# Attention and expert MoE on one core: a 128-column stationary tile for block 0's fold, and keys requested ahead of queries

## The chip, the cores and the metric

The kernel runs as one program on one core of a Trainium2 chip. The metric is the device time of one execution in microseconds (us); lower is better. The figure of the kernel before is the median of three runs.

## The reference

Block-causal attention for 8 batches of 8 heads (576 tokens, head dimension 64, blocks of 64 tokens), and behind it a mixture of 8 experts, each token through the one expert that its gate picks:

```python
scores = scale * np.matmul(q, k.transpose(0, 1, 3, 2))
mask = (pos[:, None] // 64) >= (pos[None, :] // 64)
attn = softmax(np.where(mask, scores, -1e9))
x = np.matmul(attn, v)               # heads side by side: 4608 x 512
expert_idx = np.argmax(x @ w_gate, axis=1)
for e in range(8):
    out[mask_e] = gate_w * (relu(x[mask_e] @ w1[e]) @ w2[e])
```

Everything is float32.

## The kernel before

The attention works on **pairs** of heads: 32 pairs, four to a batch. A pair's 576 queries are split into block 0 (the first 64 tokens, which see only themselves) and four tiles of 128 queries, numbered 1 to 4. The two heads of a pair lie on the two halves of the partitions.

A software pipeline runs the steps of several pairs together. The text `ORDER` lists the steps of one **turn**, each with a lag: `S4:2` in turn t is step S4 of pair t-2. Every engine executes its own steps in the order of this list; the tile framework adds the semaphore waits. A turn is one pair's worth of work; there are 32 and a few to fill and drain the pipeline. The list is written out by hand, and nothing reorders it. Letters:

- **ld** (`op_ld`, L98 to L108): three DMA requests on SP's queue, for the pair's queries `qd` (352 KB, three buffers), its keys `kd` (288 KB, two buffers) and its values `v` (352 KB, five buffers). A request is held on the queue until its buffer is free, and what stands behind it in the queue is held with it. The buffer of `qd` was last read by S0 of three pairs earlier, early in the same turn; that of `kd` by cK and lK of two pairs earlier, the latter in the turn before.
- **cK, lK, cQ, lQ**: keys and queries are split into a rounded part (`kh`, `qh`, ScalarE, that is ACT) and a rest (`kl`, `ql`, VectorE, that is DVE). cK of a pair comes late in the turn of its ld; lK and cQ come in the next turn, lQ, q0 and the scores S4 in the one after.
- **S1 to S4** (L202): scores, in three products each. S4 writes the banks `xa` and `xb`, S1 to S3 write `ya` and `yb`. `xa` and `ya` share one buffer of PSUM, as do `xb` and `yb`: S2, the first of the three in the order, waits until **E4A**, the exponentials read from `xa`, is done.
- **K, M, E**: masking and row maximum (DVE), exponentials (ACT, L234, which end with a read of the accumulator). **T** and **H**: transposes on PE (L270, L273) and their copies out of PSUM. Ta1 needs the exponentials of its pair, E3A last among them.
- **V0 to V5** (L304): products with the values, 64 columns of stationary tile for each head. V5 belongs to block 0. **O** and **O0** copy the results to SBUF.
- **F1, F2, F0** (L339, L333): the **fold**. Each multiplies the transposed output of a pair, as the stationary tile, with 144 columns: an identity, which turns the output back, and the gate's weights for the pair's rows. F1 and F2 take two tiles of 128 columns each; F0 takes block 0's 64 columns. In the trace every float32 product appears as two instructions, so F1 and F2 are four each and F0 two.
- **X, Y** (L348, L358): DVE scales the fold's results on their way to SBUF. F0 opens a new use of the PSUM bank that F1's results lie in, and so it waits until X1 and **Y1** have read them. F2 shares F0's bank.
- **z** and **y**: the router's small steps for the batch before, spread over the turns (DVE, POOL, and a few small products on PE).

The end of a turn on PE is, in order: Tk0, Tb2, F1, Tb1, Ta2, F0, F2, S2, S1, S3, Tx3, Tt0, V0, V2, and in the next turn V1, V3, V4, V5, Ta1, S0, S4.

Behind the attention, from about 370 us on, the experts' products run with an order and semaphores of their own; the change doesn't touch them. At the very start, `__init__` issues ld for pairs 0 and 1, clears constants, and runs seven products on the identity.

Of the kernel before, what the change touches and what calls it, by code (L numbers as in the profile page):

```python
# [8 lines left out]
F32 = mybir.dt.float32  # L9
# [9 lines left out]
P = 128  # L19
H = 8  # L20
S = 576
D = 64
# [14 lines left out]
FC = P + 2 * E  # L37


class Attention:  # L40
# [8 lines left out]
    def __init__(self, ctx, tc, ident, qT, kT, vt, w_gate, ends, po):  # L49
        self.tc, self.nc = tc, tc.nc  # L50
        self.qT, self.kT, self.vt = qT, kT, vt
        self.po = po

        self.ends = ends.rearrange("p (i c) -> p i c", c=P)
        self.M = qT.shape[0] * H // 2
        nc = self.nc
        cp = ctx.enter_context(tc.tile_pool(name="acst", bufs=1))
        self.raw = ctx.enter_context(tc.tile_pool(name="araw", bufs=3))
        self.rawk = ctx.enter_context(tc.tile_pool(name="arawk", bufs=2))
        self.rawv = ctx.enter_context(tc.tile_pool(name="arawv", bufs=5))  # L60
        self.spl = ctx.enter_context(tc.tile_pool(name="aspl", bufs=2))
        self.pt = ctx.enter_context(tc.tile_pool(name="apt", bufs=9))
        self.sm = ctx.enter_context(tc.tile_pool(name="asm", bufs=3))
        self.ot = ctx.enter_context(tc.tile_pool(name="aot", bufs=2))
        self.xp = ctx.enter_context(tc.tile_pool(name="axp", bufs=2))
        self.ps = ctx.enter_context(tc.tile_pool(name="psa", bufs=1, space=PSUM))
        self.ps_t = ctx.enter_context(tc.tile_pool(name="pst", bufs=2, space=PSUM))

        self.cp, self.ident = cp, ident
        self.raws, self.qs = {}, {}  # L70
        self.pb, self.sums, self.neg, self.rs = {}, {}, {}, {}
        self.bank, self.ptile, self.ph, self.oT, self.xs = {}, {}, {}, {}, {}
        self.small_bank, self.at = (None, None), {}
        self.used = {}
        self.op_ld(0)
        self.op_ld(1)
        self.zero = cp.tile([P, D], F32, tag="zero", name="zero")
        nc.vector.memset(self.zero, 0.0)

        self.h0 = [cp.tile([P, P], F32, tag=f"h0{i}", name=f"h0{i}") for i in range(2)]  # L80
        for t in self.h0:
            nc.gpsimd.memset(t, 0.0)
        self.p0 = {}

        t = self.ps_t.tile([P, 512], F32, tag="pt", name="early")
        for _ in range(7):
            nc.tensor.matmul(t[:, 0:P], ident, ident, start=True, stop=True)

        self.fold = cp.tile([P, H // 2, FC], F32, tag="fold", name="fold")
        nc.vector.memset(self.fold, 0.0)  # L90
        nc.scalar.copy(self.fold[:, :, 0:P], ident[:, None, :].to_broadcast([P, H // 2, P]))
        wg = w_gate.rearrange("(m j d) e -> j d m e", d=D, j=2)
        for j in range(2):
            nc.sync.dma_start(self.fold[D * j : D * j + D, :, P + E * j : P + E * j + E], wg[j])
# [3 lines left out]
    def op_ld(self, m):  # L98

        nc = self.nc  # L100
        b = m // 4
        qd = self.raw.tile([P, QS], F32, tag="qd", name=f"qd{m}")
        kd = self.rawk.tile([P, S], F32, tag="kd", name=f"kd{m}")
        v = self.rawv.tile([P, VS, D], F32, tag="v", name=f"v{m}")
        nc.sync.dma_start(qd, self.qT[b, m % 4])
        nc.sync.dma_start(kd, self.kT[b, m % 4])
        nc.sync.dma_start(v, self.vt[b, m % 4])
        self.raws[m] = (qd, kd, v)  # L108

# [201 lines left out]
        self.copy(engine)(t, self.banks(m, "o"))  # L311

    def op_O0(self, m, engine):
        t = self.oT[m, 1] = self.ot.tile([P, D], F32, tag="oT0", name=f"oT0{m}")
        self.copy(engine)(t, self.at["V5", m])

    def out(self, b):
        if b not in self.xs:
# [10 lines left out]
    def op_F(self, m, n):  # L329

        mm, w = self.nc.tensor.matmul, self.fold[:, m % 4]
        if n == 0:
            mm(self.part(2, m, "F0", 2 * FC, 3 * FC)[0:64], self.oT.pop((m, 1)), w, start=True, stop=True)  # L333
            return
        self.part(n, m, n, 0, 2 * FC)
        t = self.rows(m, n)
        for i in range(2):
            o = P * (2 * n - 2 + i)
            mm(t[:, i], self.oT[m, 0][:, o : o + P], w, start=True, stop=True)  # L339
# [1051 lines left out]
```

## Time and profile before

| | |
|---|---|
| median of 3 runs | 837.51 us (837.16 to 837.9) |
| profiled execution, its own time | 834.95 us |
| its span, first to last instruction | 833.2 us |
| PE busy | 812.3 us, 97% of the span |
| ACT, DVE, POOL busy | 554.4, 420.5, 355.4 us |
| mean granted clock of TensorE | 0.995 |

The span is 1.75 us shorter than the profiled execution's own time, and that execution is 2.6 us faster than the median of the runs that were only timed. Busy shares are means over two stages: the attention (to about 366 us) and the experts. In the table of rows below, "idle before" is the time in which the engine did nothing ahead of an instruction, and the name behind the arrow is what ended it; PEld is the load of a stationary tile, which can overlap products.

### The profile page before, as it was taken

The page shows a single profiled execution, that of the slowest core. Times are in us where ns is not written, and L with a number is a line of the kernel's source. Part 1 is how long each engine was busy: PE and PEld are TensorE (multiplying, and loading weights), DVE is VectorE, ACT ScalarE, POOL GpSimd, SP SyncE. Part 2 cuts the span into 40 slices and gives each one's busy share as a digit, 9 for nine tenths or more (in the row PEclk, how much of TensorE's full clock was granted, in tenths as well). Part 3 has the DMA queues.
Part 4 walks back from the last instruction along what each step waited for, and adds up shares of the span by engine and source line. Part 5 has one row for each costly group of instructions (what it writes and reads, how often), then busy time and mean ns, then how long its engine had stood idle before and what let it go on. Part 6 is the DMA issues. An engine that isn't in the chain of part 4 may idle for free.

```text
span 833.2 us, 16492 instructions
## 1 busy us (share of the span) xinstructions
PE 812.3 (97%) x5126; PEld 631.0 (76%) x5126; DVE 420.5 (50%) x1208; ACT 554.4 (67%) x1254; POOL 355.4 (43%) x390
## 2 busy tenths in 40 slices
PE   5999999999999999989999999999999999999996
PEld 4777767777777767767888888888888888888884
DVE  5677787777877877748804400045646544000000
ACT  6888988889888888834554555455546554554552
POOL 2000133222223512244855645466666655544553
PEclk8999999999999999999999999999999999999999
DMA  5225656546363529143946523246766853133212
GB/s 204 82 98 150 166 134 169 124 138 142 121 138 106 142 79 255 35 120 116 284 104 167 167 59 77 76 135 170 236 185 173 267 152 74 43 76 76 67 48 67
DMA packets 83707, 108.81 MB, mean 131 GB/s; under 512 B 45601, under 2 KB 48929, under 8 KB 83618
## 3 DMA queue, kind: packets, MB, share of 16 engines
q1 hardware_dynamic: 38082, 78.26, 31.9%
q0 software_dynamic: 7520, 19.97, 8.1%
q10 hardware_dynamic: 38016, 9.44, 6.9%
q8 instruction: 50, 0.82, 0.4%
q14 instruction: 39, 0.32, 0.1%
HBM read 76.76 MB, written 21.98 MB: 118 GB/s over the span
## 4 chain that ended last, share of the span: by engine, by line
PE 89%; DVE 2%; POOL 2%; ACT 2%; issue 1%; DMA 0%; ACTq 0%; POOLq 0%; DVEq 0%
PE py L1057 23%; PE o L936 12%; PE ph L936 12%; PE o L304 11%; PE o L339 4%; PE ya L202 4%; PE xa L202 3%; PE yb L202 2%; PE px L895 2%; PE pt L1018 2%; PE o L333 1%; ACT pb L234 1%; PE o L190 1%; DVE neg L219 1%; DVE w L1186 1%
## 5 line engine op out<-in xcount | busy, mean ns | idle before, releaser
L1057 PE MATMUL py<-w,low 128*128 (+1 forms) x912 | 226.9, 398 | 0.8 <-ACT low L1009 0.8
L1057 PEld LDWEIGHTS py<-w,low 128*128 128x128 f32 x912 | 168.8, 188 | 38.1 <-issue 1.2
L1180 DVE CAST w<-raw 128x1024 fp32r<-128x1024 f32 x60 | 48.1, 849 | 179.6 <-PE o L936 128.1
L247 POOL TENSOR_SCALAR p<-p,rs 128x64 f32<-128x64 f32 x32 | 14.2, 445 | 257.2 <-DVE rs L243 154.9
L1037 POOL TENSOR_TENSOR low<-h,low 128x512 fp32r<-128x512 f32 x72 | 107.1, 1491 | 21.2 <-ACT h L1010 21.0
L914 POOL TENSOR_TENSOR xl<-xf,xh 128x512 fp32r<-128x512 f32 x38 | 52.0, 1369 | 110.7 <-ACT xf L908 110.6
L1186 DVE TENSOR_TENSOR w<-raw,w 128x1024 fp32r<-128x1024 f32 x60 | 83.9, 1455 | 0.0
L905 ACT CAST xh<-px 128x512 fp32r<-128x512 f32 x38 | 22.3, 588 | 90.9 <-PE px L895 90.9
L936 PE MATMUL ph<-w,xh 128*128 x280 | 75.8, 393 | 0.0
L936 PE MATMUL o<-w,xh 128*128 x280 | 75.8, 393 | 0.0
L983 ACT COPY h<-ph 128x1024 uint16<-128x1024 uint16 x36 | 36.4, 1012 | 45.3 <-PE ph L936 24.0
L974 ACT ACTIVATE h<-o 128x512 f32<-128x512 f32 x37 | 22.2, 600 | 61.8 <-PE o L936 48.2
L936 PEld LDWEIGHTS ph<-w,xh 128*128 128x128 f32 x280 | 52.6, 188 | 11.9
L936 PEld LDWEIGHTS o<-w,xh 128*128 128x128 f32 x280 | 52.6, 188 | 11.7
L1081 POOL DMA_INDIRECT out<-y,idx x35 | 38.0, 1085 | 41.0 <-issue 36.8
L234 ACT ACTIVATE pb<-ya,neg 128x320 f32<-128x320 f32 (+2 forms) x93 | 48.6, 533 | 2.5 <-PE pt30x L273 1.8
L877 POOL DMA_INDIRECT xg<-xd,idx x37 | 45.1, 1220 | 10.4 <-POOL idx L873 10.4
L234 ACT ACTIVATE pb<-yb,neg 128x320 f32<-128x320 f32 (+2 forms) x93 | 49.5, 548 | 0.0
L731 POOL DMA_INDIRECT tab<-toks,posi x40 | 41.8, 1044 | 15.1 <-issue 14.6
L339 PE MATMUL o<-fold,oT 128*128 128x144 f32 x256 | 45.4, 300 | 0.9 <-ACT oT L311 0.6
L1001 ACT COPY h<-hf 128x1024 uint16<-128x1024 uint16 x36 | 43.3, 1203 | 4.1 <-DMA hf<-h 4.0
L219 DVE TENSOR_REDUCE neg<-ya 128x1 f32<-128x320 f32 (+2 forms) x93 | 44.8, 481 | 1.0 <-ACT pb L234 0.9
(965 smaller groups left out, 2122.5 us busy)
## 6 DMA issues: line engine op xcount, KB each, us to landing
raw<-w SPq DMA_DIRECT2D x60, 512.0 KB, 5.4
qd<-qT SPq DMA_DIRECT2D x32, 352.0 KB, 2.9
v<-vt SPq DMA_DIRECT2D x32, 352.0 KB, 4.4
kd<-kT SPq DMA_DIRECT2D x32, 288.0 KB, 3.8
xd<-xt SPq DMA_DIRECT2D x7, 1026.0 KB, 11.3
xd<-xg SPq DMA_DIRECT2D x9, 256.5 KB, 6.9
xg<-w SPq DMA_DIRECT2D x8, 256.0 KB, 10.8
xd<-x SPq DMA_DIRECT2D x8, 128.0 KB, 6.5
```

The source lines that it names most:

```text
L202: ins = mm(out, q[x][r, 128 * (i - 1) : 128 * i], q[y][r, o : o + w], start=n == 0, stop=n == 2, skip_group_check=True,)
L219: ins = self.nc.vector.tensor_reduce(self.neg[m][:, c : c + 1], src, AX.XY if i == 4 else AX.X, ALU.max, negate=True)
L234: ins = self.nc.scalar.activation(dst, src, AF.Exp, bias=self.neg[m][:, c : c + 1], scale=1.0, accum_out=self.sums[m][:, c : c + 1])
L304: self.nc.tensor.matmul(out[r], self.raws[m][2][:, slot], self.ph[m, bank][:, c0:c1], start=t in (0, 5), stop=t in (4, 5), skip_group_chec ...
L339: mm(t[:, i], self.oT[m, 0][:, o : o + P], w, start=True, stop=True)
L877: pool.indirect_dma_start(out=self.xg[i], out_offset=None, in_=self.xd[:, :], in_offset=bass.IndirectOffsetOnAxis(ap=self.idx[:, t : t + 1 ...
L914: pool.tensor_sub(self.xl, self.xf, self.xh).then_inc(sem["xp"], 1)
L936: m = pe.matmul(self.ph[f], x[:, P * k : P * k + P], weights(k, f, part), start=start and k == 0, stop=stop and k == 3,)
L1037: engine.tensor_sub(hl, self.hf if t < 2 else self.h[f], hh).then_inc(sem["hp"], 1)
L1057: m = pe.matmul(self.py[t % 2], h[:, c // 4, P * (c % 4) : P * (c % 4) + P], wf[:, bass.ds(off + (base + 512 * c), 512)], start=n == 0, st ...
L1180: dve.tensor_copy(hi, raw[m % nr]).then_inc(sem["wh"], 1)
L1186: dve.tensor_sub(lo, raw[m % nr], hi).then_inc(sem["wd"], 1)
```

## The change

Three things. A pair of constant SBUF tiles `o0` (128x128, cleared once by GpSimd, that is POOL) takes the place of the rotating 128x64 tile that O0 writes; O0 fills its first 64 columns. F0 takes all 128 columns of it as its stationary tile and so writes 128 rows of PSUM, of which Y0 still reads the first 64. And in `op_ld` the request for the keys goes ahead of that for the queries.

```diff
         self.h0 = [cp.tile([P, P], F32, tag=f"h0{i}", name=f"h0{i}") for i in range(2)]
-        for t in self.h0:
+        self.o0 = [cp.tile([P, P], F32, tag=f"o0{i}", name=f"o0{i}") for i in range(2)]
+        for t in self.h0 + self.o0:
             nc.gpsimd.memset(t, 0.0)
...
+        nc.sync.dma_start(kd, self.kT[b, m % 4])
         nc.sync.dma_start(qd, self.qT[b, m % 4])
-        nc.sync.dma_start(kd, self.kT[b, m % 4])
         nc.sync.dma_start(v, self.vt[b, m % 4])
...
     def op_O0(self, m, engine):
-        t = self.oT[m, 1] = self.ot.tile([P, D], F32, tag="oT0", name=f"oT0{m}")
-        self.copy(engine)(t, self.at["V5", m])
+        t = self.oT[m, 1] = self.o0[m % 2]
+        self.copy(engine)(t[:, 0:D], self.at["V5", m])
...
         if n == 0:
-            mm(self.part(2, m, "F0", 2 * FC, 3 * FC)[0:64], self.oT.pop((m, 1)), w, start=True, stop=True)
+            mm(self.part(2, m, "F0", 2 * FC, 3 * FC), self.oT.pop((m, 1)), w, start=True, stop=True)
             return
```

## Rows read from the trace of the kernel before

**Rows 1.** Busy time by stage, 100 to 200 us: us, then each engine, clock, DMA.

```profile
100.00:200.00 100.00, 99.11 (x839) 71.00 (x837) 78.02 (x299) 87.27 (x249) 29.82 (x40) 1.00 0.60 142
```

**Rows 2.** PE's waits to 360 us: total us, times, longest (the longest wait).

```profile
PE pt0a L273 <- ACT pb L234: 5.4, 1, 5.4
```

**Rows 3.** Chain that ended last, 140 to 164 us: start, us, what.

```profile
141.05 0.34 PE ya L202
...
149.38 0.49 PE o L339 x4
...
150.76 0.39 PE o L333 x2
151.15 0.69 PE o L339 x4
151.84 0.34 PE ya L202
...
163.61 0.34 PE ya L202
```

**Rows 4.** Timeline of a common turn: start, us, instruction, idle before it.

```profile
194.61 0.18 DVE L358 TENSOR_TENSOR lg<-o,rs 128x32 f32<-128x32 f32 x1
...
194.98 0.46 PE L333 MATMUL o<-fold,oT 128*64 128x144 f32 x2
...
195.57 0.22 ACT L234 ACTIVATION_READ_ACCUMULATOR pb<-xa,neg 128x1 f32 x1
...
196.05 0.18 PEld L202 LDWEIGHTS ya<-kh,qh 64*128 64x128 f32 x1
```

**Rows 5.** Timeline, DVE and PE, a turn in which Y1 is late.

```profile
106.51 0.18 DVE L358 TENSOR_TENSOR lg<-o,rs 128x32 f32<-128x32 f32 x1
...
106.84 0.43 PE L333 MATMUL o<-fold,oT 128*64 128x144 f32 x2
```

**Rows 6.** Timeline, PE, the last F1, which opens its bank.

```profile
364.94 0.61 PE L339 MATMUL o<-fold,oT 128*128 128x144 f32 x3 [0.33 <-DVE lg L358]
```

**Rows 7.** Timeline of a turn in which ACT has a router step.

```profile
337.11 0.19 ACT L234 ACTIVATION_READ_ACCUMULATOR pb<-xa,neg 128x1 f32 x1
...
337.41 0.18 PEld L202 LDWEIGHTS ya<-kh,qh 64*128 64x128 f32 x1
```

**Rows 8.** Timeline of the turn after a router step on ACT.

```profile
85.52 0.22 ACT L234 ACTIVATION_READ_ACCUMULATOR pb<-xa,neg 128x1 f32 x1
...
86.17 0.18 PEld L202 LDWEIGHTS ya<-kh,qh 64*128 64x128 f32 x1
```

**Rows 9.** Timeline, PE, Ta1 of pair 13.

```profile
158.05 0.66 PE L273 MATMUL pt13a<-ident,pb 128*128 128x128 f32 x4 [0.56 <-ACT pb L234]
```

**Rows 10.** Timeline, ACT, the same turn.

```profile
154.79 0.67 ACT L119 CAST kh<-kd 128x576 fp32r<-128x576 f32 x1 [1.79 <-DMA kd<-kT]
...
157.77 0.22 ACT L234 ACTIVATION_READ_ACCUMULATOR pb<-ya,neg 128x1 f32 x1
```

**Rows 11.** Timeline, ACT, cK in a common turn.

```profile
187.00 0.67 ACT L119 CAST kh<-kd 128x576 fp32r<-128x576 f32 x1 [0.49 <-PE yb L202]
```

**Rows 12.** Timeline, ACT, cK in the turn of pair 8.

```profile
110.48 0.67 ACT L119 CAST kh<-kd 128x576 fp32r<-128x576 f32 x1 [1.52 <-DMA kd<-kT]
```

**Rows 13.** Timeline, SP's queue: the keys that rows 10 wait for.

```profile
147.96 0.38 SPq L106 DMA_DIRECT2D kd<-kT  x1
```

**Rows 14.** Timeline of the start.

```profile
4.25 0.54 POOL L131 TENSOR_SCALAR q<-qd 128x128 f32<-128x128 f32 x1
...
4.85 0.67 ACT L119 CAST kh<-kd 128x576 fp32r<-128x576 f32 x1 [1.24 <-DMA kd<-kT]
...
5.42 0.62 ACT L116 ACTIVATE qh<-qd 128x512 fp32r<-128x512 f32 x1
...
8.58 0.67 ACT L119 CAST kh<-kd 128x576 fp32r<-128x576 f32 x1 [2.53 <-DMA kd<-kT]
```

**Rows 15.** Busy time by stage, 11.90 to 18.73 us (columns as in rows 1).

```profile
11.90:18.73 6.83, 4.22 (x23) 3.83 (x24) 3.34 (x11) 4.57 (x16) 0.00 (x0) 0.50 0.25 78
```

## The prediction

> **What bounds the kernel now.** I read the page first, then the stages, PE's waits, the chain of work that ended last, and the timeline around each touched step. In the attention PE is busy 99 us of 100, ACT 87 and DVE 78 [rows 1]. PE's longest wait is 5.4 us at the very start [rows 2]; those behind it are short. So in the steady turns PE sets the pace, and a nanosecond that its queue loses counts unless ACT or DVE ends a wait at the same place. The experts' stage behind it is bound by PE too and is not touched: it starts earlier by what the attention gains.
>
> Busy doesn't mean at peak. In the chain, F1 passes in 0.49 us for four instructions, 0.1225 each, but F0 takes 0.39 for two, and F2, the same work as F1, takes 0.69 [rows 3]. All stream 144 columns. F1 follows transposes with 128 columns of stationary tile; F0 has 64, and F2 has 128 again. The excess is 0.39 - 0.245 = 0.145 at F0 and 0.69 - 0.49 = 0.20 at F2: 0.345 us a turn at two changes of shape.
>
> The Trainium skill (TensorEngine Tiling (Array Packing), "Key Properties") says that a change of tiling mode drains TensorE. By that rule alone the change would give back the whole excess, 0.345 us a turn; the rows agree on where it lies, and the next part shows why I take less.
>
> **F0, step by step.** The copy O0 moves the same 64 columns, and F0 streams the same 144. Its wait doesn't go: it still opens the bank that Y1 reads last. In a common turn Y1 ends at 194.61 + 0.18 = 194.79, F0 starts 0.19 later and takes 0.46 to the end of its second instruction: 0.65 after Y1 [rows 4]. In a turn with Y1 late the start comes 0.15 after it (106.69 to 106.84), and F0 takes 0.43: 0.58 [rows 5]. So 0.15 is what the wait itself costs, and F0 hangs on DVE, not only on PE.
>
> With 128 columns and the wait in place, the nearest row is the last F1, which opens its bank behind a late Y: three instructions in 0.61, so two in 0.61 - 0.12 = 0.49 [rows 6], against 0.43 for the narrow one: the wide tile's load comes too late to be hidden. New F0: 0.15 + 0.49 = 0.64 after Y1. A common turn gains 0.65 - 0.64 = 0.01 there, a late one loses 0.06. F2 then follows without a change of shape and gains its 0.20. The change of shape into S2 stays. Sum: **0.21** us in a common turn, **0.14** where Y1 is late.
>
> **What comes late next.** S2 writes the buffer that E4A reads. E4A's last instruction ends at 195.79 and S2's load starts at 196.05, 0.26 later [rows 4]. The least distance that I find between such an end and PE's start is 0.06 (157.99 to 158.05, where PE did wait [rows 9, 10]), so S2 can move up by **0.20**, a hair less than the gain. In the seven turns in which ACT carries the router's exponential (the rows show the last) the end is 0.11 ahead [rows 7], and only **0.05** can be had. In the seven turns after those it is 0.43 ahead [rows 8], no limit; Y1 is late there behind a router step.
>
> Of the 32 turns, 30 lie where PE sets the pace. By kind: 14 common x 0.20 = 2.8; 7 with the router's exponential x 0.05 = 0.35; 7 after them and 2 more with Y1 late, 9 x 0.14 = 1.3. Sum **4.5 us**. Upper bound, if the wide load were hidden in spite of the wait: the same limits at S2, but 0.345 in the nine, 2.8 + 0.35 + 3.1 = 6.3. Lower bound, if the excess isn't the change of shape: only the later wide load is left, -0.06 x 30 = 1.8 us slower.
>
> ACT behind S2: it waits 0.49 us for PE ahead of cK in a common turn [rows 11]; PE's gain of 0.20 eats less than half. DVE is less busy than ACT [rows 1]. I cost the two extra clears on POOL at nothing: they run at the start while ACT waits 1.24 us for keys [rows 14]; without that cover they would delay the identity and PE's warm-up, which feeds nothing.
>
> The rule that speaks against the change is in the Trainium skill, TensorE: Matmul & The Clock Gate, "LDWEIGHTS (loading the stationary operand)": the load's time goes with the columns, P / 1.2 ns, so 64 more cost some 53 ns, an estimate from that page. If both loads of F0 were exposed in 30 turns that is 3.2 us, where my sum has 1.8 from the rows, and counts it already in each turn.
>
> **Keys first, steady turns.** In two turns cK waits for the keys' DMA: 1.79 us and 1.52 us [rows 10, 12], where a common turn waits 0.49 for PE [rows 11]. ACT is 1.30 and 1.03 us late. In the first, Ta1 then waits for ACT [rows 9], and the turn takes 163.61 - 151.84 = 11.77 us against 151.84 - 141.05 = 10.79: 0.98 lost, 0.32 absorbed [rows 3]. By the same absorption the other loses at most 0.71; Ta1's wait there is short, so I take 0.5. Together 1.5 us.
>
> With keys first, the request no longer stands behind the queries', which wait for S0 early in the turn. It needs lK of the turn before, which the trace has done before S2 begins, at 141.05 there [rows 3], so it could go out some 6.9 us ahead of its 147.96 [rows 13]; it needed 154.79 - 147.96 = 6.8 us to land amid the batch's row writes, and is wanted at 154.79 - 1.30 = 153.5. Landing near 141.05 + 6.8 = 147.9 leaves 5 us to spare, unless the writes, issued just before, hold it. Behind it on the queue stand queries and values, neither delayed: the queries still go when S0 is done, and are read a turn later. Bounds 0 and 1.7; I take **1.3**.
>
> **Keys first, start.** ACT begins with cK of pair 0 at 4.85, waiting for keys requested second; the queries, requested first, had landed by 4.25 (POOL reads them then) [rows 14]. Swapped, cK starts near 4.25 and cQ near 4.9, when the queries land, against 5.42: 0.5 earlier. Pair 1's keys, for which ACT waits 2.53 us [rows 14], come earlier likewise, and the exponentials behind that copy with them: some 0.9 at the end of PE's 5.4 us wait. But PE then works at the lower granted clock, 0.50 of full, which is 1.2 GHz, until 18.73 [rows 15]; if the rise comes at the same moment, time won ahead of it is worth half. Bounds 0 and 1.0; I take **0.7**.
>
> **Sum.** 4.5 + 1.3 + 0.7 = 6.5 us. The profiled execution (834.95, of it 833.2 span, 1.75 around it) would take 828.45, its span 826.7. The median of the runs shown is 2.55 above the profiled one; the same 6.5 off it: 837.5 - 6.5 = **831.0 us**.
>
> **Rivals.**
>
> - *The wide load hides behind the transposes after all.* F1 shows 0.1225 per instruction throughout [rows 3]; against it stands the wait for Y1, seen in common and late turns alike. Fold 6.3, keys 2.0: 837.5 - 8.3 = 829.2 us. This is what the rule on draining, named above, comes to under the limit at S2.
> - *Late keys don't set those turns, or the row writes hold the keys as before, and the start's gain is lost to the clock.* For it: the keys would queue right behind the writes. Then only the fold counts: 837.5 - 4.5 = 833.0 us.
> - *The fold gains nothing: the excess is the wait for Y1, not the shape, and the load's lateness is added.* Against it: F2 waits for nothing new and still takes 0.20 more than F1. Fold -1.8, keys +2.0: 837.3 us, no change.
> - *Slower.* The same mechanism, at F0 in each turn, with keys that bring nothing: 837.5 + 1.8 = 839.3 us. It decides if F2 keeps 0.69 in the chain while F0 grows from 0.39 to 0.45. By the page's figure for the load it would be 840.7.
>
> **How the numbers follow.** The forecast has 0.62, with its own range of 829 to 832.5; the first rival 0.10, the second 0.16, the third 0.08, slower 0.04. A measurement of this kernel can tell about 0.2%, 1.7 us, from no change. Forecast and first two rivals are faster by more (0.88, with a little of the third: 0.89), the third within (0.07), the last slower (0.04). The range of 827.5 to 834.0 holds the first three with the bounds of keys and start (the best of all, 6.3 + 1.7 + 1.0, is 828.5); it leaves out 0.12 and the tails.
>
> **What the profile after would show.** F0 as 128*128, 0.64 after Y1; F2 at 0.49 in the chain; the first F2 instruction as short as the others; S2 within 0.05 to 0.1 of E4A's end in common turns, which says that ACT has become the limit there. ACT's waits for kd's DMA gone behind the start; PE's first long wait ending some 0.9 us sooner. The prediction is wrong if F2 keeps 0.69, if F0 ends later than 0.7 after Y1, if ACT's gap ahead of cK closes to nothing in common turns, or if cK waits for keys as long as now.

## The result, and the profile after

Median of four runs 829.75 us (828.45 to 832.52), beside 837.34 (835.52 to 837.9, four runs) for the kernel before: 7.6 us less. The ratio over all runs, which is not quite that of the two medians, is 0.9919 with a 95% interval of 0.9897 to 0.9941. Forecast were 831.0 us and a range of 827.5 to 834.0. A second series of the same kernel (`again`, below) gave 0.99.

The profiled execution took 832.52 us (span 830.8), the longest of its four, so I compare stretches of the two traces, not their ends. From the second S2 to the last one that ORDER times (31.63 to 342.73) the attention takes 311.1 us; before it was 316.2 (32.13 to 348.35). This stretch holds 29 of the forecast's 30 turns; the one ahead of it went from 10.78 to 10.56. The common turn went from 10.77 to 10.58 us.

Busy time by stage of the kernel after, columns as in [rows 1]:

```profile
100.00:200.00 100.00, 99.70 (x869) 73.89 (x866) 79.41 (x302) 89.27 (x256) 28.90 (x39) 1.00 0.60 145
```

PE is still busy throughout; ACT rose from 87 to 89 us of 100, because the same work is done in less time. The chain that ended last, where [rows 3] had 0.49, 0.39 and 0.69 for F1, F0 and F2:

```profile
136.28 0.49 PE o L340 x4
...
137.67 0.37 PE o L334 x2
138.04 0.49 PE o L340 x4
138.53 0.35 PE ya L203
```

F2 now passes in F1's 0.49. A common turn on the timeline, against [rows 4]:

```profile
190.80 0.18 DVE L359 TENSOR_TENSOR lg<-o,rs 128x32 f32<-128x32 f32 x1
...
191.12 0.48 PE L334 MATMUL o<-fold,o 128*128 128x144 f32 x2
...
191.76 0.22 ACT L235 ACTIVATION_READ_ACCUMULATOR pb<-xa,neg 128x1 f32 x1
...
192.03 0.18 PEld L203 LDWEIGHTS ya<-kh,qh 64*128 64x128 f32 x1
```

Y1 ends at 190.98. F0 starts 0.14 later and ends 0.62 after Y1; S2's load starts 1.05 after Y1, where it was 1.26, and 0.05 after E4A's end (191.98), where it was 0.26. The turn that carries the router's exponential, and the one after, against [rows 7] and [rows 8]:

```profile
73.88 0.19 ACT L235 ACTIVATION_READ_ACCUMULATOR pb<-xa,neg 128x1 f32 x1
...
74.12 0.18 PEld L203 LDWEIGHTS ya<-kh,qh 64*128 64x128 f32 x1 [0.31 <-ACT pb L235]
...
84.45 0.22 ACT L235 ACTIVATION_READ_ACCUMULATOR pb<-xa,neg 128x1 f32 x1
...
84.94 0.18 PEld L203 LDWEIGHTS ya<-kh,qh 64*128 64x128 f32 x1
```

The distance to E4A is 0.05 in the first (before 0.11) and 0.27 in the second (before 0.43). The turn that ends at the first of these S2s went from 10.77 to 10.74, the one that ends at the second from 10.94 to 10.82, and the next from 10.78 to 10.56.

The timeline of ACT and SP, against [rows 10 to 13]: cK in the two turns with late keys (108.37 and 151.37), the queue ahead of the second, and cK in a common turn (183.17):

```profile
108.37 0.67 ACT L120 CAST kh<-kd 128x576 fp32r<-128x576 f32 x1 [0.84 <-PE yb L203]
...
136.32 0.61 SPq L582 DMA_DIRECT2D xd<-xt  x1
...
138.69 0.75 SPq L106 DMA_DIRECT2D kd<-kT  x1
...
151.37 0.67 ACT L120 CAST kh<-kd 128x576 fp32r<-128x576 f32 x1 [0.89 <-PE pt12x L274]
...
183.17 0.67 ACT L120 CAST kh<-kd 128x576 fp32r<-128x576 f32 x1 [0.29 <-PE yb L203]
```

In the second the keys are requested 9.3 us sooner than at 147.96 (6.5 us, counted from the turn's S2), but the batch's row write `xd<-xt` (1 MB) was issued 2.4 us ahead of them on the same queue. The row writes' packets (2052 bytes each) run from 137.39 to 149.93, the keys' own (2304 bytes each) begin only at 145.57, and the semaphore on which cK waits for them moves last at 151.29: 12.6 us after the request, and just before cK starts. So the view's name for what ended this wait, PE, is not the whole of it. The forecast had them landed 6.8 us after the request. Counted from the turn's S2, cK starts 2.3 us behind it (151.37 - 149.11), where it was 3.0 (154.79 - 151.84) and a common turn has 1.7. The two turns took 10.75 and 11.02, before 11.35 and 11.78.

The start, against [rows 2], [rows 14] and [rows 15]: PE's longest wait, in the view of waits, the first copies on the timeline, and the busy time at the lower clock:

```profile
PE pt0a L274 <- ACT pb L235: 5.7, 1, 5.7
```

```profile
3.85 0.67 ACT L120 CAST kh<-kd 128x576 fp32r<-128x576 f32 x1 [0.23 <-DMA kd<-kT]
4.67 0.63 ACT L117 ACTIVATE qh<-qd 128x512 fp32r<-128x512 f32 x1 [0.16 <-DMA qd<-qT]
...
8.10 0.67 ACT L120 CAST kh<-kd 128x576 fp32r<-128x576 f32 x1 [2.79 <-DMA kd<-kT]
```

```profile
11.82:18.65 6.83, 4.64 (x25) 4.25 (x26) 3.44 (x9) 4.52 (x17) 0.00 (x0) 0.50 0.41 137
```

cK of pair 0 starts 1.0 us sooner, cQ 0.75, cK of pair 1 0.48. PE's wait grew, because it begins sooner; it ends at 14.01 against 14.51. S2 of the first turn comes only 0.29 sooner.

One thing stands against the gain. At the experts' start PE waits 2.56 us for `xl`, where the trace before had 0.3, and the stretch around its end has a granted clock of 0.50, 1.2 GHz (a row of PE's waits before; after, a row of the timeline and one of busy time by stage):

```profile
PE ph L936 <- POOL xl L914: 0.3, 1, 0.3
```

```profile
398.00 1.22 PE L937 MATMUL ph<-w,xl 128*128 x2 [2.56 <-POOL xl L915]
```

```profile
397.51:400.92 3.41, 2.92 (x7) 2.34 (x8) 3.41 (x3) 0.42 (x1) 3.41 (x3) 0.50 0.88 266
```

The experiments return to it.

### The profile page after: what moved, and what is told of

It is laid out like the page before. It is cut to its first block, busy times and chain, and to the rows that moved or that the text cites. A ratio compares the mean times of both kernels' runs of the same rounds, so it can differ in the third digit from the quotient of the medians.

```text
span 830.8 us, 16466 instructions
## 1 busy us (share of the span) xinstructions
PE 808.1 (97%) x5126; PEld 634.0 (76%) x5126; DVE 420.8 (51%) x1208; ACT 554.8 (67%) x1254; POOL 357.0 (43%) x392
## 4 chain that ended last, share of the span: by engine, by line
PE 87%; issue 3%; POOL 2%; ACT 2%; DMA 1%; DVE 1%; POOLq 1%; DVEq 0%; SPq 0%; ACTq 0%
PE py L1058 23%; PE o L305 12%; PE ph L937 12%; PE o L937 12%; PE ya L203 6%; PE xa L203 3%; PE o L340 3%; PE px L896 2%; PE pt L1019 2%; PE o L334 1%; ACT pb L235 1%; POOL tab L732 1%; PE o L191 1%; DMA out<-y,idx 0%; PE o L1359 0%
## 5 line engine op out<-in xcount | busy, mean ns | idle before, releaser
L1038 POOL TENSOR_TENSOR low<-h,low 128x512 fp32r<-128x512 f32 x72 | 105.2, 1464 | 24.7 <-ACT h L1011 24.7
L1082 POOL DMA_INDIRECT out<-y,idx x35 | 39.8, 1138 | 41.0 <-issue 37.0
L220 DVE TENSOR_REDUCE neg<-yb 128x1 f32<-128x320 f32 (+2 forms) x93 | 41.9, 478 | 3.3 <-ACT pb L235 1.3
```

What stands on the lines that cost most here:

```text
L220: ins = self.nc.vector.tensor_reduce(self.neg[m][:, c : c + 1], src, AX.XY if i == 4 else AX.X, ALU.max, negate=True)
L1038: engine.tensor_sub(hl, self.hf if t < 2 else self.h[f], hh).then_inc(sem["hp"], 1)
```

## The experiments

Theory: the fold gives some 4 us through F2's change of shape and is held by E4A at S2; the keys give something of 1 to 2 us by removing two late landings. Rivals: the keys carry most of it; or they carry nothing. All kernels compute the whole reference. Three series ran, each on one chip beside its own runs of the kernel before: medians 841.41 us (23 runs) in the first, 840.92 (17) in the second, 839.99 (10) in the third; the second and third ran on the same chip. The table puts them together: the ratio to the kernel before over all runs, ACT's wait for the keys' DMA behind the start (total, times, longest, as the view of ACT's waits has it), and the stretch from the second S2 to the last, both in the one profiled execution.

| kernel | median us | ratio (95%) | wait for keys, us | stretch, us |
|---|---|---|---|---|
| before, first profile | | | 3.3, 2, 1.8 | 316.2 |
| `before_again` (one run) | 844.59 | | 8.9, 3, 4.4 | 323.3 |
| `again` | 833.15 | 0.99 (0.9872 to 0.9928) | 3.4, 2, 1.8 | 312.8 |
| `fold_only` | 839.11 | 0.997 (0.9951 to 0.999) | 8.2, 5, 3.7 | 317.8 |
| `keys_only` | 836.11 | 0.9932 (0.9907 to 0.9957) | 2.2, 2, 1.3 | 315.4 |
| `keys_start` | 841.5 | 0.9977 (0.9951 to 1.0004) | 10.0, 5, 4.1 | 320.0 |
| `keys_early` | 829.6 | 0.9877 (0.985 to 0.9904) | none | 310.8 |
| `both` | 830.39 | 0.9877 (0.9851 to 0.9902) | none | 309.7 |
| `f0_with_v` | 838.95 | 0.9976 (0.9952 to 1.0001) | 1.1, 2, 0.8 | 315.8 |
| `narrow_keys_early` | 835.07 | 0.9942 (0.9924 to 0.996) | none | 315.0 |
| `narrow_f2_first` (one run) | 831.6 | | none | 313.8 |

**First series: the change once more, and its parts.** `again` is the changed kernel.

> The changed kernel once more, for a second profile. In its first profile the attention ends 5.6 us sooner than before (the first product behind it, sxl, at 360.6 against 366.2), but PE then waits 2.56 us for xl at 398 where it waited 0.29 before, and the granted clock falls there for 3.4 us. Theory: that wait is a matter of one execution, and the attention's 5.6 us is the change; then this profile has S2 of the 30th turn again near 342.7 and no such wait, a span near 828, and the time lies near 829.7. Rival: the wait belongs to the change (the experts start at another moment against their weights' DMA); then it is here again, and the span is near 830.8.

833.15 against 841.41: 8.3 us. At the experts' start there was no long wait for `xl`. But keys were late in two turns, 11.72 and 11.76 us long, and ACT waited for them as long as in the first profile of the kernel before (3.3 us, two times):

```profile
ACT kh L120 <- DMA kd<-kT: 3.4, 2, 1.8
```

So the swap doesn't always remove the late landings.

`fold_only` keeps the queries first:

```diff
-        nc.sync.dma_start(kd, self.kT[b, m % 4])
         nc.sync.dma_start(qd, self.qT[b, m % 4])
+        nc.sync.dma_start(kd, self.kT[b, m % 4])
```

> The 128-column tile for block 0's fold, with queries requested ahead of keys as before. Theory: a common turn takes 10.58 us as in the changed kernel, against 10.77; the two turns with late keys keep their wait of some 1.5 to 1.8 us for kd's DMA and take 11.2 and 11.6; the start is as before (first Ta1 at 14.5). Some 4.2 us of the gain, 833 us. Rival: the keys carry most of the gain, and the fold alone gives under 2 us: above 835.

The common turn is 10.58, as in the full change, but the time is only 2.3 us under the kernel before. The view of ACT's waits has late keys in five turns:

```profile
ACT kh L120 <- DMA kd<-kT: 8.2, 5, 3.7
```

One turn takes 16.02 us, another 12.40. Late keys alone don't explain why the gain is under the fold's 4 us, since the kernel before has them too: whether the fold's shorter turns make them later is not shown.

`keys_only` is the kernel before with the requests swapped, so the 64-column tile stays:

```diff
+        nc.sync.dma_start(kd, self.kT[b, m % 4])
         nc.sync.dma_start(qd, self.qT[b, m % 4])
-        nc.sync.dma_start(kd, self.kT[b, m % 4])
```

> Keys requested ahead of queries, with the 64-column tile as before. Theory: common turns 10.77 as before, the two turns with late keys shorter by 0.4 to 0.6 us each, first Ta1 at 14.0 instead of 14.5 and 0.3 us kept of that at the first S2 (21.07 against 21.36): 1.3 us in all, 836.0 us. Rival: over 3 us, below 834.5, with the fold's part smaller by as much.

5.3 us faster, with the common turn at its old 10.78. So by the medians the keys gave more than the fold here, though the two intervals just overlap; "something of 1 to 2 us" fell. ACT's waits:

```profile
ACT kh L119 <- DMA kd<-kT: 2.2, 2, 1.3
```

`keys_start` has the fold, and keys first for the first two pairs alone:

```diff
+        pair = [(qd, self.qT[b, m % 4]), (kd, self.kT[b, m % 4])]
+        for dst, src in pair[::-1] if m < 2 else pair:
+            nc.sync.dma_start(dst, src)
```

> The changed kernel, but keys go ahead of queries for pairs 0 and 1 alone, whose loads stand ahead of everything; all later pairs as before. Theory: the start as in the changed kernel (first Ta1 at 14.0, first S2 at 21.1), the two turns with late keys as before the change (11.2 and 11.6): 1.0 us slower than the changed kernel, 830.8. Rival: the early request of later pairs' keys is worth nothing, since the batch's row writes hold them either way: then it equals the changed kernel within 0.3 us in the profile's turns.

A plain miss: 841.5 us, and no gain of the start can be seen (PE's first wait ends at 14.51, S2 comes at 21.59). The waits for keys are back, 10.0 us in five turns. What the swap is worth lies mainly in the steady turns; from `fold_only` the intervals can't tell it.

**Second series: how late are the keys of the kernel before?** `before_again` is the kernel before, for one more profile.

> The kernel before, unchanged, for a second profile beside those of its variants. In the profiles so far the turns whose keys come late grow with the wait of cK for kd's DMA: in the kernel with the fold alone 3.7 and 2.3 us of wait and turns of 16.0 and 12.4 us, with PE's granted clock at half for 6.8 us inside the first. Theory: the kernel before has the same in most executions, and its first profile (waits of 1.5 and 1.8 us, turns of 11.35 and 11.78, no fall of the clock) was a lucky one: then here waits above 2.5 us, one turn of 13 us or more, a span of 836 or more. Rival: the fold makes the late keys later (its shorter turns ask for them sooner against the same row writes), and the kernel before stays near 11.4 and 11.8.

First the timeline of ACT and PE, then ACT's waits, then busy time by stage (columns as in [rows 1]):

```profile
113.77 0.67 ACT L119 CAST kh<-kd 128x576 fp32r<-128x576 f32 x1 [4.43 <-DMA kd<-kT]
...
115.48 0.83 PE L304 MATMUL o<-ph8x,v 128*64 128x256 f32 x4 [2.35 <-ACT ph8x L285]
```

```profile
ACT kh L119 <- DMA kd<-kT: 8.9, 3, 4.4
```

```profile
113.80:115.75 1.95, 0.27 (x2) 0.20 (x4) 0.36 (x1) 1.95 (x6) 0.00 (x0) 1.00 0.14 42
115.77:119.17 3.40, 3.33 (x24) 2.84 (x22) 2.33 (x6) 3.19 (x12) 0.00 (x0) 0.51 0.01 1
```

This is the reading that the first profile didn't allow. cK waits 4.43 us, the copy of pair 8's transposes stands behind it on ACT, PE stands behind that for 2.35 us, and then works 3.4 us at a granted clock of 0.51, the lower of the two levels. The three turns take 14.97, 14.27 and 11.43 us where 10.77 to 10.94 are usual: 8.3 us lost against the 10.8 that `narrow_keys_early`, below, has in each of them, and 1.5 in the profile that the forecast was made from. The second of them has a fall of clock of 3.4 us as well, from 163.6. A fall of clock behind such a wait stands in the traces of `fold_only` and `keys_start` too (6.83 us long in both), and in none of `after`, `again`, `keys_only` and `keys_early` between 20 and 360 us. This execution was 3.7 us slower than the median of the kernel's 17 runs beside it, so 8.3 us is not the usual loss; 4.6 us is my estimate for a median run, if late keys are all that sets the two apart.

The same trace shows whether the long wait for `xl` at the experts' start belongs to the change:

```profile
PE ph L936 <- POOL xl L914: 2.3, 1, 2.3
```

It stands here in the kernel before, so it doesn't come from the change.

`keys_early` is the full change, but the keys have three buffers and a step of their own at the turn before, ahead of the batch's row writes on the queue:

```diff
-        self.rawk = ctx.enter_context(tc.tile_pool(name="arawk", bufs=2))
+        self.rawk = ctx.enter_context(tc.tile_pool(name="arawk", bufs=3))
...
+    def op_kd(self, m):
+        kd = self.keys[m] = self.rawk.tile([P, S], F32, tag="kd", name=f"kd{m}")
+        self.nc.sync.dma_start(kd, self.kT[m // 4, m % 4])
...
-M1A:3 ld:0 V1:4 V3:4 ...
+M1A:3 kd:-1 ld:0 V1:4 V3:4 ...
```

> The changed kernel with a third buffer for keys and their request a whole turn earlier, so ahead of the row writes that hold it (it needs 12.6 us to land behind them). Theory: cK never waits for DMA behind the start, its gap is 0.30 to 0.52 us in every turn, the 9th and 13th turn (107 and 151 us) come down to some 10.6 to 10.8 us; against the changed kernel's own 0.6 to 2.3 us of late turns that is a gain of 1 to 2 us. Rival: the row writes' traffic itself slows those turns, or the request, made earlier, now holds queries and values behind it: no gain.

829.6, a ratio of 0.9877. The timeline of ACT in the turn that was the second late one:

```profile
150.48 0.67 ACT L123 CAST kh<-kd 128x576 fp32r<-128x576 f32 x1 [0.29 <-issue]
```

The two late turns are now 10.72 and 10.76 us, and ACT waits nowhere for keys behind the start. (The third buffer and the place on the queue came together; which of them is needed was not separated.) The stretch is 2.0 us shorter than in `again`; in the times the two kernels' intervals overlap.

`both` adds one move to it: the router's exponential, z1, behind E4A.

```diff
-... Y1:4 z4:0 z1:0 E4A:2
+... Y1:4 z4:0 E4A:2 z1:0
```

> As the one with a third buffer for keys, and the router's exponential put behind E4A in ACT's order instead of ahead of it. Theory: E4A is what S2 waits for in common turns, 0.05 us ahead of its load, and in the seven turns with the router's exponential it keeps S2 at 1.21 us after Y1 instead of 1.05. With the exponential out of the way S2 comes 1.05 after Y1 there too: 0.16 x 7 = 1.1 us more. Rival: the exponential only moves the wait (Hb1 or cQ behind it, or the router's chain on DVE that reads it): under 0.3 us.

Where 1.21 us lay between Y1 and S2 in those seven turns there are now 1.05, as in the others, with E4A's end (73.52) 0.06 ahead of S2's load:

```profile
73.30 0.22 ACT L238 ACTIVATION_READ_ACCUMULATOR pb<-xa,neg 128x1 f32 x1
...
73.58 0.18 PEld L206 LDWEIGHTS ya<-kh,qh 64*128 64x128 f32 x1
```

The stretch loses 1.1 us. The time can't tell it from `keys_early`.

`f0_with_v` keeps the narrow tile and the swap, and moves F0 behind V2, among products of 64 columns:

```diff
-Ta2:3 z0:0 F0:4 F2:4 ... Y0@D:4 ...
+Ta2:3 z0:0 F2:4 ...
-... V0:3 V2:3 Y2:4
+... V0:3 V2:3 F0:4 Y2:4 Y0@D:4
```

> Keys first as in the changed kernel, but the fold of block 0 as a 64-column tile again and moved on PE from ahead of F2 to behind V2, among products that have 64 columns of stationary tile too (Y0 moved behind it). No change of shape is added and no load is wide, and the stretch from Y1 to S2 has only F2 left. Theory: S2 can't use this, since E4A ends 0.05 ahead of it already; F0's 0.25 us now lengthen the stretch from S3 to Ta1 instead. Common turns 10.80 us, S2's load within 0.06 of E4A's end; some 5 to 6 us slower than the changed kernel. Rival: PE's work alone sets the turn; then common turns stay at 10.58 or fall under it, and the time is that of the changed kernel or better.

The common turn is 10.83, longer than the 10.78 of `keys_only`, and its time, 838.95, is no better. S2 can't come sooner than E4A lets it: with F0 gone from ahead of it, its load still starts 0.05 after E4A's end (52.71), in common turns and router turns alike.

```profile
52.49 0.22 ACT L235 ACTIVATION_READ_ACCUMULATOR pb<-xa,neg 128x1 f32 x1
...
52.76 0.18 PEld L203 LDWEIGHTS ya<-kh,qh 64*128 64x128 f32 x1 [0.40 <-ACT pb L235]
```

F0's time ahead of S2 was saved and couldn't be used there, and behind V2 it was paid again: 0.25 us in the common turn, against the 10.58 of the wide tile. The timeline shows that this is F0 without its excess:

```profile
45.77 0.29 PE L334 MATMUL o<-fold,oT 128*64 128x144 f32 x1
...
45.89 0.29 PE L334 MATMUL o<-fold,oT 128*64 128x144 f32 x1
46.01 0.59 PE L305 MATMUL o<-ph2a,v 128*64 128x512 f32 x1
```

Between products of its own shape the narrow F0 passes in 0.24 us (45.77 to 46.01), where it took 0.39 in the chain between wide ones.

**Third series: the fold by itself, with keys that are never late.** `narrow_keys_early` is `keys_early` with the 64-column tile.

```diff
...
-            mm(self.part(2, m, "F0", 2 * FC, 3 * FC), self.oT.pop((m, 1)), w, start=True, stop=True)
+            mm(self.part(2, m, "F0", 2 * FC, 3 * FC)[0:64], self.oT.pop((m, 1)), w, start=True, stop=True)
```

> The kernel with the third buffer for keys and their early request, with the 64-column fold of the kernel before. Against the run with the same keys and the 128-column fold this leaves the fold alone, with no late keys in either. Theory: common turns 10.77 against 10.59, the stretch from the second S2 to the last some 4.2 us longer (310.8 there, 315.0 here), the time 0.5% above it: 0.9927 of before against 0.9877, some 834 us where that one has 829.6. Rival: PE's gain in the turns is given back behind the attention, and the time is within 1 us of it.

835.07, 0.9942, against 0.9877 with the wide tile; the intervals don't touch. The stretch is 315.0 against 310.8: the fold is worth 4.2 us there. (The medians lie 5.5 us apart, from two series on one chip, with intervals 3 and 4.5 us wide.) The loads that open and end the stretch, in `keys_early`, then in `narrow_keys_early`:

```profile
31.33 0.18 PEld L206 LDWEIGHTS ya<-kh,qh 64*128 64x128 f32 x1
...
342.13 0.18 PEld L206 LDWEIGHTS ya<-kh,qh 64*128 64x128 f32 x1
```

```profile
31.95 0.18 PEld L205 LDWEIGHTS ya<-kh,qh 64*128 64x128 f32 x1
...
346.92 0.18 PEld L205 LDWEIGHTS ya<-kh,qh 64*128 64x128 f32 x1
```

`narrow_f2_first` leaves the tile narrow and changes the order alone, so that F0 no longer stands between two products of 128 columns:

```diff
-Ta2:3 z0:0 F0:4 F2:4 ...
+Ta2:3 z0:0 F2:4 F0:4 ...
```

> As narrow_keys_early, with F2 ahead of F0: the 64-column tile stays, but only its place changes. Theory: the excess belongs to the change of shape between neighbours. F2 follows transposes of its own shape and loses its 0.20 excess, but it opens the bank behind Y1 and its wide load is late; F0 keeps a change of shape on either side. From Y1's end to S2's load 1.20 us in common turns, against 1.26 with F0 first and 1.05 with the wide tile; common turns 10.71. Rival: the excess of F2 belongs to its place ahead of S2 or to the bank, not to what stands before it; then F2 still takes 0.69 in the chain and the common turn 10.77 or more.

The chain of a common turn:

```profile
41.31 0.62 PE o L342 x4
41.93 0.39 PE o L336 x2
42.32 0.34 PE ya L205
```

From Y1's end to S2 it takes 1.19 us, between the 1.26 of the narrow tile in its old place and the 1.05 of the wide one; the common turn is 10.72. F0 keeps its 0.39, though it no longer waits for Y1: a change of shape still lies ahead of it. F2 has 0.62. It now opens the bank behind Y1, and its first two instructions start 0.20 apart, as those of the wide F0 do in the changed kernel, where a stream has 0.1225; the rest of the 0.13 over F1's 0.49 is not shown. With `f0_with_v`, and with F2's 0.49 in the changed kernel at its old place and in its old bank, the excess follows the change of shape and not the place.

## Why the prediction was right, and where its size was off

**F0, step by step: right.** F0 ends 0.62 after Y1 (0.64 forecast), F2 takes 0.49 in the chain, S2 comes 0.21 sooner. Two changes of shape made the 0.345 us of excess: without them F2 runs like F1 and a narrow F0 passes in 0.24 among the values' products (`f0_with_v`), and with the one ahead of F0 left in, `narrow_f2_first` shows F0 with its 0.39. The Trainium skill (TensorEngine Tiling (Array Packing), "Key Properties") says that a change of mode drains TensorE; the traces agree in direction. Taking that rule alone, which gives back 0.345 us, would have put S2 0.92 after Y1; S2 comes 1.05 after it, because the wide load behind Y1 is exposed and E4A is in the way.

The Trainium skill's rule that spoke against the change, on the load's time (TensorE: Matmul & The Clock Gate, "LDWEIGHTS (loading the stationary operand)"), shows only behind that wait. The trace has the wide F0's two instructions start 0.20 apart, where a stream has 0.1225. I read these 0.08 us as the part of the load that isn't hidden; F2's load, with no wait ahead of it, costs nothing that shows.

**What comes late next: right.** S2's load stands 0.05 behind E4A's end in common turns and in turns with the router's exponential, 0.27 in the turns after, as worked out. `both` took the cap away in seven turns, and its stretch is 1.1 us shorter (0.16 x 7); `f0_with_v` ran into the same limit from the other side.

**The fold's sum: right.** 4.5 forecast over 30 turns. In the trace after, 5.1 us of the stretch less 1.25 for the two late turns (next point) leaves 3.9 for 29 turns, 4.1 with the turn ahead of it. `keys_early` against `narrow_keys_early` shows 4.2, and 4.4 with that turn.

**Keys first, steady turns: right in mechanism, too small in size.** The term of 1.3 us, with an upper bound of 1.7, was read from one execution with waits of 1.79 and 1.52 us. Between the two first traces it came out: the two turns lost 1.5 us before (against `narrow_keys_early`) and 0.3 after (against `keys_early`), so 1.25 were gained. But `before_again` loses 8.3 us to the same cause, `fold_only` and `keys_start` wait 8.2 and 10.0 us, and `keys_only` gained 5.3 us in the first series. The bound was that of one execution, not of the kernel. In these traces cK waits more than 3 us five times; each time PE runs dry, and in four of the five it then works at the lower clock, which the first profile didn't contain.

**"5 us to spare, unless the writes hold it": the writes hold it.** The keys landed 12.6 us after their request in the late turn, so they come hardly in time or, in `again`, still make cK wait 1.8 us. In `again` cK waits for keys as long as in the first profile before, one of the prediction's own signs of being wrong: the keys don't land with 5 us to spare. `keys_early`, whose request stands ahead of the writes, has none. The second rival had this part right and its conclusion, that keys don't count, wrong: `keys_only` refutes it.

**Keys first, start: too large in the first pair of traces.** 0.7 forecast, 0.29 seen at the first S2. The copies do start 0.5 to 1.0 sooner, but PE's wait ends 0.5 sooner and not 0.9. The other half of the working held: the clock rises at 18.65 where it rose at 18.73, so of the 0.50 won ahead of it 0.08 count in full and 0.42 by half, which makes 0.29. With the swap that wait ends between 13.43 (`both`) and 14.51 (`keys_start`), without it between 14.15 (`fold_only`) and 14.53 (`before_again`). The first S2 comes at 20.9 in the mean of the nine profiles with the swap (20.5 to 21.6) and at 21.4 in the three without (21.2 to 21.7): some 0.5 us, with a scatter as large.

**The sum: right, in part by luck.** 6.5 us forecast, 7.6 measured beside the same runs, 8.3 in the first series. Between the two first traces the last S2 comes 5.6 us sooner (348.35 to 342.73): 4.1 for the fold, 1.25 for the late keys, 0.3 for the start. Those are the forecast's terms, each at or under its size. The other 2 us of the timed gain stand in neither of these traces. That they are late keys in other executions of the kernel before is what `before_again` and `keys_only` suggest; no profile of the timed runs shows it. The forecast knew nothing of them, and the number fell well inside the range because what it left out was no larger than this.

**Left open: the experts' start.** The wait of 2.3 to 2.7 us for `xl` is in seven of the twelve profiles, those of `before_again`, `fold_only` and `narrow_keys_early` among them, and in none of `again`, `keys_early`, `both`, `narrow_f2_first` and the first of before. It stands with either tile and either order of the requests, so it isn't of this change. In the trace after, the part behind the last S2 took 3.2 us longer than before, and 2.3 of that are this wait; it may be why the profiled execution of after was the longest of its four. In the trace after, POOL's drain ahead of it takes 9.96 us and in the first trace of before 7.8. What makes the wait come or not was not tried.

## What to carry to other kernels

A product whose stationary tile is of another shape than its neighbours' cost more here than its own time: look in the chain for the same operation at two durations (0.49 and 0.69 here), and count the changes of shape between them; then ask which buffer's reader waits next, for that caps the gain. A load that is late in two turns of one profile is a sample, not a price: take a second profile of the kernel before, and ask whether the engine that sets the pace runs dry behind it: then a turn here lost as much as the wait (4.2 us for one of 4.43) or more (5.3 for one of 3.69). A request that stands behind another's long wait on a queue goes first, and if bulk writes are on that queue, ahead of those too, with a buffer more.

## What the runs showed of the hardware that I had not expected

A read of 288 KB took 12.6 us to land behind a 1 MB write on the same queue, and, counted from the turn's S2, a request 6.5 us earlier landed only 0.7 us earlier (2.2 us behind that S2, where it was 2.9). After PE had stood nearly idle (0.27 us busy of 1.95), the granted clock was 0.51 for the 3.4 us that followed, so a late DMA was paid twice; one wait of 1.72 us on PE, in `keys_start`, had no such fall behind it. And one kernel on chips of one kind waited 3.3 us for its keys in one execution and 8.9 in another.
